# Gated attention and mixture of experts on one core: the order of ranking, indexed stores and first products

## The chip, the cores and the metric

The kernel runs on one core of a Trainium2 chip. The metric is the time of one execution in microseconds (us) of the device, the median of several runs. Engines go by the names of the profile: PE (TensorE matmuls), PEld (its weight loads), DVE (VectorE), ACT (ScalarE), POOL (GpSimd) and SP (SyncE, which here only issues DMAs). Each engine works through its own list of instructions in order; it stops at an instruction whose inputs or whose buffer are not ready, and everything behind it in that list stops too.

## The reference

For 4 batches and 8 heads, 768 steps, a state of 48 x 48 is decayed and read:

```python
f = 1.0 / (1.0 + np.exp(-f_logit))
for t in range(S):
    state = f[:, :, t, :, None] * state + np.einsum('bhd,bhe->bhde', k[:, :, t], v[:, :, t])
    y[:, :, t] = np.einsum('bhd,bhde->bhe', q[:, :, t], state)
```

Its 3072 rows of 384 numbers go to a mixture of 8 experts with 1024 hidden units:

```python
logits = x @ w_gate                       # 8 logits a row
expert_idx = np.argmax(logits, axis=1)    # one expert a row
for i in range(N):                        # in the order of the rows
    e = expert_idx[i]
    if counts[e] < capacity:
        disp[e, counts[e]] = x[i]; pos[i] = counts[e]; counts[e] += 1; keep[i] = True
h = np.maximum(np.einsum('ecd,edf->ecf', disp, w1), 0.0)
y = np.einsum('ecf,efd->ecd', h, w2)
out[i] = gate_w[i] * y[expert_idx[i], pos[i]]   # for the rows kept, gate_w the softmax weight
```

## The kernel before, in words

**Attention in slots.** The 3072 rows are 24 blocks of 128, six to a batch. A prologue readies the first ones, then slots 0 to 24 follow. The order within a slot is written by hand and holds for all five engines. In slot `n`, in this order:

- `keys_pe(n)` turns the keys of block `n` (PE, psT buffers), ACT copies them out as `kn`; `y_out` copies the result of block `n-1` (ACT).
- `scores_pe(n+1)` (PE, psA), which ACT copies to `AT` and POOL masks with two affine selects.
- `kq_pad(n+3)` copies loaded keys and queries into a padded tile `kqp` (POOL in slots 0 to 6, ACT later); `kq_in(n+2)` transposes them (PE, psT), and DVE multiplies them by decays into `kT` and `qT`.
- `f_in` transposes the gates of two blocks in every odd slot (PE, two psF buffers, one for each block). In slots 9 and 15 it stands behind `inter`, otherwise ahead of it.
- `inter(n)` (PE) reads the carried state `S`; `update(n)` (PE) makes the new one, which DVE adds up (`U`) and POOL decays into the next `S` (`carry`).
- `decay(n+3)` and `decay_back(n+3)` are two scans on DVE over the psF buffer of block `n+3`. The second one writes `Rq`, and the buffer is free when it ends.
- `rows_pe(n-1)` (PE) turns the result into rows with the 8 logits beside them, as products with `identc`, which holds an identity and the gate columns; ACT copies them into a ring of 12 blocks.
- `values(n)` (PE) adds the block's own part.

`load` issues on SP the transfers of k and q together (`kq`, three buffers), of v, and of f for two blocks. `late_constants` loads the gate columns into `identc` with four small DMAs, and the capacity.

**Ranking.** The rows of a group of blocks (`GROUPS`) are given their expert together: POOL adds partial logits (`choose_sum`), DVE finds the largest (`choose_max`) in the slot after the group's last block is in rows; one slot later POOL multiplies by `desc`, DVE finishes the one-hot choice (`choose_first`, into `tally`), PE ranks the rows with matmuls of ones and a triangle (`rank_pe`), and DVE makes from that the row numbers `ri` (`pick` and `put`). The first two groups have six blocks each, the others three or one.

**Stores by index.** `flush_scatter` sends one ranked block of 128 rows to the experts' buffer `disp` in HBM: an indirect DMA that POOL issues. `SCATTERS` says how many a slot; `AHEAD` names four slots that have one more, ahead of the masks. From slot 20 on one more follows each `rows_copy`. The rows of blocks 0 to 14 for expert 0 are read back first: after the store of block 14, SP loads `xg0`.

**The first expert inside attention.** In the last slots `early_prep` transposes `xg0` (PE, psF), and ACT and DVE split it into `x0h` and `x0l`. `early_pe` makes the eight first-layer products of 256 rows (nine matmuls each; psF for most, psT for two, psA for the last) and `early_out` takes them out (`hh` on ACT, then `hl` on DVE). The table `EARLY` says in which slot, and at which of three places in it. The second layer follows, then a second small expert and seven sorted by size, with the weights of each loaded and split meanwhile. `QUARTERS` says where POOL splits parts of the first expert's weights (`w1l`).

The functions that the diff touches:

## Time and profile before

| what | value |
|---|---|
| runs | 384.35, 383.87, 384.09 us; median 384.09 |
| profiled execution | 385.96 us; span from first to last instruction 383.5 us |
| instructions | 10139 |
| PE busy | 371.7 us, 97% of the span |
| DVE busy | 212.2 us, 55% |
| ACT busy | 201.9 us, 53% |
| POOL busy | 178.7 us, 47% |
| granted PE clock | 0.998 |

The profile is of one execution, and all durations in this text are of that one. A row of its timeline has the start in us, the length, the engine and source line, the operation with output and inputs, how many were merged into the row, and in brackets how long the engine sat idle just before and which instruction's end released it. The ends of matmuls are modelled: a PE that waits inside a group of matmuls can look busy. Slots are told apart by `rows_pe`, line 539: that of slot 1 starts at 22.76, of slot 7 at 51.79, of slot 13 at 81.28, of slot 19 at 113.38. The first matmul of the second layer (line 1019) starts at 143.88.

### The profile page before, as it was taken

The page shows a single profiled execution, that of the slowest core. Times are in us where ns is not written, and L with a number is a line of the kernel's source. Part 1 is how long each engine was busy: PE and PEld are TensorE (multiplying, and loading weights), DVE is VectorE, ACT ScalarE, POOL GpSimd, SP SyncE. Part 2 cuts the span into 40 slices and gives each one's busy share as a digit, 9 for nine tenths or more (in the row PEclk, how much of TensorE's full clock was granted, in tenths as well). Part 3 has the DMA queues.
Part 4 walks back from the last instruction along what each step waited for, and adds up shares of the span by engine and source line. Part 5 has one row for each costly group of instructions (what it writes and reads, how often), then busy time and mean ns, then how long its engine had stood idle before and what let it go on. Part 6 is the DMA issues. An engine that isn't in the chain of part 4 may idle for free.

```text
span 383.5 us, 10139 instructions
## 1 busy us (share of the span) xinstructions
PE 371.7 (97%) x4007; PEld 347.1 (91%) x4007; DVE 212.2 (55%) x482; ACT 201.9 (53%) x425; POOL 178.7 (47%) x260
## 2 busy tenths in 40 slices
PE   8889999999999999999999999999999999999994
PEld 7789899888878899998899989999999999999994
DVE  4988889878889867534943343225225235222310
ACT  3556668876768632552834553545454464462311
POOL 6664545677767853254253430370290281292012
PEclk9999999999999999999999999999999999999999
DMA  8979999999883423679386174175156036211001
GB/s 154 213 156 225 230 241 228 242 226 248 205 228 101 146 97 120 231 220 321 126 273 195 29 243 124 43 239 180 42 184 227 23 125 210 76 60 41 16 22 40
DMA packets 83323, 60.87 MB, mean 159 GB/s; under 512 B 65671, under 2 KB 77829, under 8 KB 83268
## 3 DMA queue, kind: packets, MB, share of 16 engines
q1 hardware_dynamic: 79476, 50.13, 50.6%
q0 software_dynamic: 3520, 9.92, 6.9%
q8 instruction: 33, 0.54, 0.6%
q14 instruction: 22, 0.18, 0.2%
q10 hardware_dynamic: 272, 0.10, 0.1%
HBM read 49.42 MB, written 11.43 MB: 159 GB/s over the span
## 4 chain that ended last, share of the span: by engine, by line
PE 74%; issue 9%; DMA 5%; POOL 4%; SPq 3%; ACT 3%; DVE 1%; POOLq 1%; ACTq 0%
PE psM L1190 15%; PE psA L763 11%; PE psM L763 9%; PE psM L1019 7%; PE psA L539 5%; PE psY L518 5%; PE psA L420 5%; PE psY L464 3%; DMA raw<-in_moe_w_dram 3%; PE psA L484 2%; PE psT L360 2%; PE psT L447 2%; PE psT L1161 2%; PE psF L763 2%; PE psF L360 1%
## 5 line engine op out<-in xcount | busy, mean ns | idle before, releaser
L320 POOL DMA_INDIRECT out_dram<-yo,g_ti x30 | 30.0, 998 | 100.5 <-ACT yo L1206 40.3
L144 POOL TENSOR_TENSOR w2l<-raw,w2h 128x768 fp32r<-128x768 f32 x28 | 51.2, 1856 | 39.4 <-ACT w2h L135 39.4
L770 DVE SCALAR_TENSOR_TENSOR hl<-psA,hh 128x224 fp32r<-128x224 f32 (+8 forms) x33 | 18.5, 559 | 48.6 <-ACT hh L769 48.6
L144 DVE TENSOR_TENSOR w1l<-raw,w1h 128x1024 fp32r<-128x1024 f32 x21 | 25.5, 1223 | 24.5 <-ACT w1h L135 24.5
L135 ACT ACTIVATE w1h<-raw 128x1024 fp32r<-128x1024 f32 x24 | 25.3, 1062 | 25.4 <-DMA raw<-in_moe_w_dram 25.3
L1019 PE MATMUL psM<-w2h,hh 128*128 128x384 f32 (+2 forms) x112 | 37.6, 342 | 0.0
L1019 PE MATMUL psM<-w2l,hh 128*128 128x384 f32 (+2 forms) x112 | 37.5, 338 | 0.0
L1019 PE MATMUL psM<-w2h,hl 128*128 128x384 f32 (+2 forms) x112 | 37.4, 337 | 0.0
L770 DVE SCALAR_TENSOR_TENSOR hl<-psM,hh 128x224 fp32r<-128x224 f32 (+7 forms) x32 | 17.8, 562 | 31.1 <-ACT hh L769 31.1
L1190 PE MATMUL psM<-hh,w2h 128*128 128x440 f32 (+3 forms) x96 | 34.1, 355 | 0.0
L1190 PE MATMUL psM<-hl,w2h 128*128 128x440 f32 (+3 forms) x96 | 34.1, 355 | 0.0
L1190 PE MATMUL psM<-hh,w2l 128*128 128x440 f32 (+3 forms) x96 | 33.8, 352 | 0.0
L430 POOL TENSOR_SCALAR_AFFINE_SELECT AT<-AT 128x512 f32<-128x512 f32 x48 | 29.4, 636 | 8.5 <-ACT AT L426 8.3
L135 ACT ACTIVATE w2h<-raw 128x768 fp32r<-128x768 f32 x32 | 27.1, 847 | 9.9 <-DMA raw<-in_moe_w_dram 8.7
L320 POOL DMA_INDIRECT disp<-rows,ri x24 | 25.6, 1065 | 13.1 <-issue 3.5
L380 DVE TENSOR_TENSOR_SCAN Suf<-psF,direv 112x511 f32<-112x511 f32 x24 | 29.1, 1211 | 3.8 <-PE psF L360 3.8
L769 ACT ACTIVATE hh<-psA 128x224 fp32r<-128x224 f32 (+8 forms) x33 | 16.2, 492 | 27.1 <-PE psA L763 20.5
L763 PE MATMUL psM<-xh,w1h 128*128 128x480 f32 (+6 forms) x84 | 29.7, 354 | 0.0
L763 PE MATMUL psA<-xh,w1h 128*128 128x480 f32 (+6 forms) x84 | 29.7, 353 | 0.1
L763 PE MATMUL psM<-xl,w1h 128*128 128x480 f32 (+6 forms) x84 | 29.7, 354 | 0.0
L763 PE MATMUL psA<-xh,w1l 128*128 128x480 f32 (+6 forms) x84 | 29.4, 350 | 0.0
L394 DVE TENSOR_TENSOR_SCAN Rq<-psF,d 112x512 f32<-112x512 f32 x24 | 29.4, 1224 | 0.0
(238 smaller groups left out, 958.6 us busy)
## 6 DMA issues: line engine op xcount, KB each, us to landing
raw<-in_moe_w_dram SPq DMA_DIRECT2D x24, 512.0 KB
raw<-in_moe_w_dram SPq DMA_DIRECT2D x32, 384.0 KB
ld_kq<-in_k_dram SPq DMA_DIRECT2D x24, 192.0 KB
ld_kq<-in_q_dram SPq DMA_DIRECT2D x24, 192.0 KB
ld_v<-in_v_dram SPq DMA_DIRECT2D x24, 192.0 KB
ld_f<-in_f_logit_dram SPq DMA_DIRECT2D x11, 384.0 KB
xg<-disp SPq DMA_DIRECT2D x6, 589.5 KB
xg<-disp SPq DMA_DIRECT2D x3, 393.0 KB
```

The costliest lines, as they stand in the source:

```text
L135: return nc.scalar.activation(hi, raw, AF.Copy)
L144: engine.tensor_tensor(lo[cs], raw[cs], hi[cs].bitcast(F32), op=ALU.subtract)
L320: ins = nc.gpsimd.indirect_dma_start(out=dst, out_offset=bass.IndirectOffsetOnAxis(ap=idx, axis=0), in_=rows, in_offset=None, bounds_check ...
L380: nc.vector.tensor_tensor_scan(out=_view(Suf[:R], m - 1, [[-1, m]]), data0=_view(F, m, [[-1, m]]), data1=_view(direv[:R], m - 1, [[-1, m]] ...
L394: nc.vector.tensor_tensor_scan(out=Rq[:R], data0=F, data1=d1[:R], initial=0.0, op0=ALU.mult, op1=ALU.max)
L420: nc.tensor.matmul(pas[s][:, p], kTs[n][r, p], qTs[n][r, p], start=True, stop=True)
L430: nc.gpsimd.affine_select(AT[:, s], AT[:, s], pattern=[[0, NP], [1, C]], compare_op=ALU.is_ge, fill=0.0, base=0, channel_multiplier=-1)
L518: nc.tensor.matmul(py[b][64 * g : 64 * g + m, a, :], vt[:, 2 * p + s, :m], AT[:, s, p, :], start=(first(n) and a == 0), stop=(a == NP // 2 ...
L763: nc.tensor.matmul(ph[:, :T], a[:, c, fs], x[:, c, :T], start=(n == 0), stop=(n == 3 * DT - 1))
L770: nc.vector.scalar_tensor_tensor(out=hl[:, :T], in0=ph[:, :T], scalar=0.0, in1=hh[:, :T].bitcast(F32), op0=ALU.max, op1=ALU.subtract)
L1019: nc.tensor.matmul(py[:n], x[:, ks], a[:, ft], start=(ft == 0 and m == 0), stop=(ft == FT - 1 and m == 2))
L1190: nc.tensor.matmul(pys[c][:, :T], a[:, ft, cs], x[:, :T], start=(ft == 0 and n == 0), stop=(ft == FT - 1 and n == 2))
```

## The change

The first twelve blocks are ranked in three groups of four. Blocks are stored one a slot from slot 7 on (two in slot 20), and the extra stores ahead of the masks are gone. The load of `xg0` stands a slot later, and with it the transposes and products of the first expert. In slot 0 the copy of key and query block 3 goes behind `carry`, `f_in(4)` ahead of `kq_in(3)` in slot 1, the gate columns are loaded earlier and the capacity later.

```diff
-    GROUPS = ((0, 6), (6, 6), (12, 3), (15, 3), (18, 3), (21, 1), (22, 1), (23, 1))
-    RT = 6
+    GROUPS = ((0, 4), (4, 4), (8, 4), (12, 3), (15, 3), (18, 3), (21, 1), (22, 1), (23, 1))
+    RT, RING = 4, 12
...
-    QUARTERS = {9: (0, 3), 12: (0, 1), 13: (1, 2), 14: (1, 2), 20: (2, 3), 21: (2, 1)}
-    SCATTERS = {9: 1, 10: 1, 11: 1, 12: 1, 13: 1, 14: 1, 15: 1, 16: 1, 17: 1, 18: 2, 19: 1, 20: 0}
-    AHEAD = (15, 17, 19, 21)
+    QUARTERS = {9: (0, 1), 10: (0, 1), 11: (0, 2), 12: (1, 2), 15: (1, 2), 18: (2, 2), 21: (2, 2)}
+    SCATTERS = {n: 1 for n in range(NT - 3)}
...
         for s in range(2):
-            copied = nc.scalar.activation(AT[:, s], pas[s], AF.Copy)
-        if n - 1 in AHEAD:
-            flush_scatter(copied.ins)
+            nc.scalar.activation(AT[:, s], pas[s], AF.Copy)
...
     def rows_parts(n, px):
-        t, c = divmod(n, RT)
-        if t not in parts_of:
-            parts_of[t] = abuf.tile([P, RT, NP, NE], F32, name="parts", bufs=1)
-        nc.scalar.activation(parts_of[t][:, c], px[:, :, 2 * D :], AF.Copy)
+        nc.scalar.activation(ring_parts[:, n % RING], px[:, :, 2 * D :], AF.Copy)
...
     EARLY = {
-        (NT - 3, 1): ((early_prep, 0),),
-        (NT - 3, 2): ((early_prep, 1), (early_prep, 2)),
-        (NT - 2, 0): ((early_pe, 0), (early_pe, 1)),
...
+        (NT - 2, 0): ((early_prep, 0),),
+        (NT - 2, 1): ((early_prep, 1),),
+        (NT - 2, 2): ((early_prep, 2),),
+        (NT - 1, 0): ((early_pe, 0), (early_pe, 1)),
...
     def prologue():
...
         load("v", 1)
+        late_constants()
         keep_busy(4)
...
         load("v", 2)
-        late_constants()
         load("kq", 5)
...
     def loads_of(n):
         load("v", n + 3)
-        if n < PAD_ACT:
+        if 0 < n < PAD_ACT:
             load("kq", n + 6)
         if n == 0:
             load("f", 4)
+        if n == 2:
+            nc.sync.dma_start(cap_i, capacity.bitcast(I32).partition_broadcast(P))
...
     def slot(n):
...
-        if fn and n < PAD_ACT:
+        if 0 < n < PAD_ACT:
             kq_pad(n + 3)
...
+        if n == 1:
+            f_in(4)
         if kqn:
             kq_in(n + 2)
...
-        if n == 1:
-            f_in(4)
         loads_of(n)
...
         if keyed:
             carry(n)
+        if n == 0:
+            kq_pad(3)
+            load("kq", 6)
...
-        if n == NT - 5:
+        if n == NT - 4:
             ins = nc.sync.dma_start(xg0, dispv[0, : T_FIRST[0]].rearrange("(k p) w -> p k w", p=P))
```

**POOL and SP in slots 0 and 1.** The rows of POOL from the copy of block 2 (into `kqp0`) to the masks of AT(2); `S1` is the state that `inter(1)` reads. Before:

```order
L401 COPY kqp0_122<-ld_kq2_105 128x16x48
L430 AFFINE_SELECT AT_346<-AT_346 128x512 x2
L401 COPY kqp1_124<-ld_kq0_103 128x16x48
L430 AFFINE_SELECT AT_417<-AT_417 128x512 x2
L504 TENSOR_TENSOR S1_149<-U_438,pendall_189 112x4x48
L401 COPY kqp0_122<-ld_kq1_104 128x16x48
L430 AFFINE_SELECT AT_503<-AT_503 128x512 x2
```

After:

```order
L399 COPY kqp0_122<-ld_kq2_105 128x16x48
L426 AFFINE_SELECT AT_351<-AT_351 128x512 x2
L426 AFFINE_SELECT AT_416<-AT_416 128x512 x2
L500 TENSOR_TENSOR S1_149<-U_435,pendall_189 112x4x48
L399 COPY kqp1_124<-ld_kq0_103 128x16x48
L399 COPY kqp0_122<-ld_kq1_104 128x16x48
L426 AFFINE_SELECT AT_512<-AT_512 128x512 x2
```

The copy of block 3 (into `kqp1`) has moved from in front of the masks of AT(1) to behind the state. On SP the gate columns move ahead of `kq` 4 (buffer 1) and `v` 2, and the capacity goes to slot 2. Before, from the load of v 1 on:

```order
L199 DMA ld_v1_108<-in_v_dram 128x8x48
L204 DMA ld_kq1_104<-in_k_dram 64x8x96
L204 DMA ld_kq1_104<-in_q_dram 64x8x96
L199 DMA ld_v2_110<-in_v_dram 128x8x48
L276 DMA identc_151<-in_moe_w_gate_dram 48x2x8 x4
L277 DMA cap_i_168<-in_moe_capacity_dram 128x2
L204 DMA ld_kq2_105<-in_k_dram 64x8x96
```

After:

```order
L198 DMA ld_v1_108<-in_v_dram 128x8x48
L275 DMA identc_151<-in_moe_w_gate_dram 48x2x8 x4
L203 DMA ld_kq1_104<-in_k_dram 64x8x96
L203 DMA ld_kq1_104<-in_q_dram 64x8x96
L198 DMA ld_v2_110<-in_v_dram 128x8x48
L203 DMA ld_kq2_105<-in_k_dram 64x8x96
```

**DVE from slot 9 to slot 10.** From the second scan of block 12 (`Rq`) to that of block 13, whose end frees the psF buffer for `f_in` of slot 11. Before:

```order
L394 SCALAR_TENSOR_TENSOR Rq_1478<-psF_1425,d1_145 112x512
L409 TENSOR_TENSOR kT_1532<-psT_1514,Suf0_141 112x512
L409 TENSOR_TENSOR qT_1534<-psT_1515,Rq_1478 112x512
L498 TENSOR_TENSOR U_1562<-psA_1553,S0_147 112x192
L380 SCALAR_TENSOR_TENSOR Suf1_143<-psF_1426,direv_138 112x511
L388 RECIPROCAL d1_145<-Suf1_143 112x4
L389 TENSOR_TENSOR pendall_189<-psF_1426,Suf1_143 112x4
L394 SCALAR_TENSOR_TENSOR Rq_1585<-psF_1426,d1_145 112x512
```

After, with the choice of blocks 4 to 7 in front of kT:

```order
L392 SCALAR_TENSOR_TENSOR Rq_1481<-psF_1430,d1_145 112x512
L575 TENSOR_REDUCE r_m_1483<-rows_195 128x4
L577 TENSOR_TENSOR r_w_1485<-rows_195,r_m_1483 128x32
L583 TENSOR_REDUCE r_wm_1522<-r_w_1485 128x4
L585 TENSOR_TENSOR tally_1118<-r_w_1485,r_wm_1522 128x32
L407 TENSOR_TENSOR kT_1543<-psT_1525,Suf0_141 112x512
L407 TENSOR_TENSOR qT_1545<-psT_1526,Rq_1481 112x512
L494 TENSOR_TENSOR U_1580<-psA_1564,S0_147 112x192
L634 TENSOR_TENSOR r_sel_1582<-psA_1564,tally_1118 128x4x8
L378 SCALAR_TENSOR_TENSOR Suf1_143<-psF_1431,direv_138 112x511
L386 RECIPROCAL d1_145<-Suf1_143 112x4
L387 TENSOR_TENSOR pendall_189<-psF_1431,Suf1_143 112x4
```

Four instructions of the choice and one of the ranking now stand between the two scans, as they did in slots 8 and 14 before.

**PE at the end of slot 22.** `tally` in the last columns is the choice of block 21. Before, from the end of the third product of the first expert to the start of the fourth:

```order
L763 MATMUL psF<-x0l,w1h 128x256
L763 MATMUL psF<-x0h,w1l 128x256
L677 LDWEIGHTS onesb
L677 MATMUL psT<-base_178,onesb 128x8
L678 LDWEIGHTS onesb
L678 MATMUL psT<-tally,onesb 128x8
L684 LDWEIGHTS tri
L684 MATMUL psT<-tally,tri 128x8
L960 LDWEIGHTS onesb
L960 MATMUL psT<-flb,onesb 128x1
L763 MATMUL psF<-x0h,w1h 128x256
```

After, from the end of `values(22)`:

```order
L514 MATMUL psY<-AT,ld_v_114 64x128
L710 MATMUL psF<-ident,xg_85 128x128 x2
L667 LDWEIGHTS onesb
L667 MATMUL psT<-base_178,onesb 128x8
L668 LDWEIGHTS onesb
L668 MATMUL psT<-tally,onesb 128x8
L674 LDWEIGHTS tri
L674 MATMUL psT<-tally,tri 128x8
L947 LDWEIGHTS onesb
L947 MATMUL psT<-flb,onesb 128x1
L745 MATMUL psF<-x0h,w1h 128x256
```

Between `values(22)` and this ranking there is now a pair of transposes of `xg0` where there was a product of nine matmuls, and the first product comes behind the ranking.

More of the change, by code (lines that the diff above doesn't have):

```diff
@@ L276, in late_constants @@
                 nc.sync.dma_start(identc[64 * g : 64 * g + D, b::2, 2 * D :], gates_of[b, g ^ b])
-        nc.sync.dma_start(cap_i, capacity.bitcast(I32).partition_broadcast(P))
     ohc = const.tile([P, NE], BF16, name="ohc")
@@ L412 @@
     MS = (64, D)
-    pus, ATs, kns, pys, yTs, marks, parts_of = {}, {}, {}, {}, {}, {}, {}
+    pus, ATs, kns, pys, yTs, marks = {}, {}, {}, {}, {}, {}
     def scores_pe(n):
@@ L541, in rows_pe @@
         return px
-    ring = abuf.tile([P, 2 * RT, W], F32, name="rows", bufs=1)
+    ring = abuf.tile([P, RING, W], F32, name="rows", bufs=1)
     def row_at(n):
-        return ring[:, n % (2 * RT)]
+        return ring[:, n % RING]
     def rows_at(g, m):
-        c = g % (2 * RT)
+        c = g % RING
         return ring[:, c : c + m]
     def rows_copy(n, px):
-        if n >= 2 * RT:
+        if n >= RING:
             nc.gpsimd.tensor_copy(row_at(n)[:, DM + NE : W], tokid[:, n : n + 1])
@@ L560, in rows_copy @@
         marks[n].append(m)
+    ring_parts = abuf.tile([P, RING, NP, NE], F32, name="parts", bufs=1)
     def rows_parts(n, px):
[L563 to L566 removed]
+        nc.scalar.activation(ring_parts[:, n % RING], px[:, :, 2 * D :], AF.Copy)
     def group(g, m):
[L569 to L570 removed]
+        c = g % RING
+        return ring_parts[:, c : c + m], rows_at(g, m)[:, :, DM : DM + NE]
     def choose_sum(g, m):
@@ L593, in sum_parts @@
     def sum_parts(g, m):
-        t, c = divmod(g, RT)
-        nc.vector.tensor_reduce(
-            out=rows_at(g, m)[:, :, DM : DM + NE],
-            in_=parts_of[t][:, c : c + m].rearrange("r c a e -> r c e a"),
-            axis=AX.X,
-            op=ALU.add,
-        )
+        part, L = group(g, m)
+        nc.vector.tensor_reduce(out=L, in_=part.rearrange("r c a e -> r c e a"), axis=AX.X, op=ALU.add)
     def rows_logits(n, px):
@@ L687, with flush_scatter @@
     queue, early_ins, slot_now, ri_of = [], [], {"n": 0}, {}
-    def flush_scatter(behind=None):
+    def flush_scatter():
         if queue:
@@ L693, in flush_scatter @@
             ins = scatter(disp, ri_of.pop(n), row_at(n), NV * RPE - 1, ("disp", "late") if late else ("disp",))
-            if behind is not None:
-                tc.add_manual_dep(
-                    ins,
-                    behind.name,
-                    mybir.DependencyInfo(mybir.DependencyClass.Sync, mybir.DependencyReason.DATA),
-                    reason="not during the transposes",
-                )
             if not late:
@@ L740 @@
     EARLY = {
-        (NT - 3, 1): ((early_prep, 0),),
-        (NT - 3, 2): ((early_prep, 1), (early_prep, 2)),
-        (NT - 2, 0): ((early_pe, 0), (early_pe, 1)),
-        (NT - 2, 1): ((early_out, 0), (early_out, 1)),
-        (NT - 2, 2): ((early_pe, 2),),
-        (NT - 1, 0): ((early_out, 2), (early_pe, 3)),
-        (NT - 1, 1): ((early_out, 3), (early_pe, 4)),
-        (NT - 1, 2): ((early_out, 4), (early_pe, 5)),
-        (NT, 0): ((early_out, 5),),
-        (NT, 2): ((early_pe, 6), (early_pe, 7), (early_out, 6)),
+        (NT - 2, 0): ((early_prep, 0),),
+        (NT - 2, 1): ((early_prep, 1),),
+        (NT - 2, 2): ((early_prep, 2),),
+        (NT - 1, 0): ((early_pe, 0), (early_pe, 1)),
+        (NT - 1, 1): ((early_out, 0), (early_pe, 2)),
+        (NT - 1, 2): ((early_out, 1), (early_out, 2), (early_pe, 3), (early_pe, 4)),
+        (NT, 0): ((early_out, 3), (early_pe, 5)),
+        (NT, 1): ((early_out, 4),),
+        (NT, 2): ((early_pe, 6), (early_pe, 7), (early_out, 5), (early_out, 6)),
     }
@@ L845, in slot @@
             pas = scores_pe(n + 1)
-        if fn and n < PAD_ACT:
+        if 0 < n < PAD_ACT:
             kq_pad(n + 3)
         if n == 3:
-            nc.gpsimd.tensor_copy(ring[:, :, DM + NE : W], tokid[:, : 2 * RT].unsqueeze(2))
+            nc.gpsimd.tensor_copy(ring[:, :, DM + NE : W], tokid[:, :RING].unsqueeze(2))
         while half:
```

2 lines of the change are left out of this document (removed).

## The prediction

> **What bounds the kernel now.** I first read the busy time of TensorE in four stretches of the span, to learn whether an engine or a wait sets the end. Columns: stretch, its length, then busy time and instructions of PE, PEld, DVE, ACT and POOL, granted clock, DMA share, GB/s.
>
> ```profile
> 23.50:144.00 120.50, 117.96 (x2406) 105.18 (x2402) 102.01 (x223) 84.35 (x210) 77.39 (x128) 1.00 0.86 203
> 144.00:200.00 56.00, 55.91 (x335) 52.08 (x335) 32.00 (x103) 27.00 (x54) 22.75 (x20) 1.00 0.66 217
> 200.00:330.00 130.00, 130.00 (x715) 124.69 (x714) 49.27 (x97) 64.16 (x112) 45.65 (x33) 1.00 0.44 142
> 46.62:75.75 29.13, 28.80 (x641) 25.96 (x641) 25.97 (x50) 23.50 (x57) 16.22 (x28) 1.00 1.07 235
> 75.75:107.41 31.66, 30.52 (x648) 26.79 (x648) 27.41 (x58) 23.29 (x57) 23.98 (x42) 1.00 0.97 231
> ```
>
> From the end of attention (144 us) TensorE is busy without a gap, so whatever moves that moment moves the end of the kernel by as much; the change edits nothing behind it. Before it TensorE is missing 2.5 us in the open and more inside its groups: slots 13 to 18 (last row) hold the same work as slots 7 to 12 (the row above), but for 0.2 us of ranking, and take 2.53 us longer. So I read the timeline of attention engine by engine, and take each part of the change by one question: does TensorE arrive earlier or later at its next instruction.
>
> **Part 1, slots 0 and 1.** Four places in the timeline of slot 1, and the DMA engines' busy tenths from 20 to 40 us in steps of 0.5 us:
>
> ```profile
> 21.05 0.67 PE L464 MATMUL psY<-qT,S 48*64 48x128 f32 x16 [0.54 <-POOL S L504]
> 22.76 0.93 PE L539 MATMUL psA<-identc,yT 112*64 112x104 f32 x16 [0.45 <-DMA identc<-in_moe_w_gate_dram]
> 18.53 0.83 POOL L401 COPY kqp<-ld_kq 128x768 f32<-128x768 f32 x1 [3.01 <-DMA ld_kq<-in_q_dram]
> 18.02 2.36 SPq L276 DMA_DIRECT2D identc<-in_moe_w_gate_dram  x4
> 20.42 1.54 SPq L277 DMA_DIRECT2D cap_i<-in_moe_capacity_dram  x1
> DMA  5310000699999999999999992696599999999999
> 26.80 0.69 DVE L409 TENSOR_TENSOR kT<-psT,Suf 112x512 f32<-112x512 f32 x1 [1.39 <-PE psT L360]
> ```
>
> TensorE waits 0.54 us for the carried state S, because POOL first copies `kq` block 3 (0.83, itself released only by its DMA) and masks AT. It waits 0.45 us more for the gate columns, whose four small loads SP issues at 18.02. SP spends 3.9 us on these and the capacity, while the DMA engines run dry from 20.5 to 23.5. The change issues the gate loads three loads earlier, moves the capacity to slot 2, and puts the copy of block 3 behind S; `f_in(4)` fills TensorE while that copy runs. Both waits go: -1.0, and I take -1.1 for the shorter queue. What is pushed back: `kq` 4 and `v` 2 go behind the four gate loads (2.36 us), so POOL's copies of blocks 3 and 4 now stand together in front of AT(2); these are needed only in slot 2, where VectorE has 1.39 us idle (last row), and the filled DMA hole gives the time back. `kq` 6 now waits for the copy of block 3 and stands behind `f` 4, a load of 384 KB more; its copy is due in slot 3, and the same hole covers it. If that cover fails, half the gain goes: from -1.2 to -0.4.
>
> **Part 2, groups of four.** Three groups issue 18 ranking matmuls for 16, at 0.04 us: +0.1. What matters is VectorE. The chain that chooses an expert is now in front of kT in slots 6, 10 and 14 (before: 8 and 14). In slots 9 and 15 the code puts the next transposes of f behind `inter`; slots 7 and 11, which now follow a choice, keep them ahead. They write two psF banks, and the second is free when Rq of the slot before ends. Rows: Rq(8), kT(8), Rq(9) and the transposes of slot 7, then the same of slots 10 and 11, then the choice in slot 8 from its first to its last instruction.
>
> ```profile
> 43.49 1.22 DVE L394 TENSOR_TENSOR_SCAN Rq<-psF,d 112x512 f32<-112x512 f32 x1
> 45.60 0.69 DVE L409 TENSOR_TENSOR kT<-psT,Suf 112x512 f32<-112x512 f32 x1 [0.89 <-PE psT L360]
> 48.53 1.22 DVE L394 TENSOR_TENSOR_SCAN Rq<-psF,d 112x512 f32<-112x512 f32 x1
> 50.15 0.61 PE L360 MATMUL psF<-ident,pf 64*112 64x64 f32 x16
> 64.03 1.22 DVE L394 TENSOR_TENSOR_SCAN Rq<-psF,d 112x512 f32<-112x512 f32 x1
> 65.60 0.69 DVE L409 TENSOR_TENSOR kT<-psT,Suf 112x512 f32<-112x512 f32 x1 [0.35 <-PE psT L360]
> 68.63 1.22 DVE L394 TENSOR_TENSOR_SCAN Rq<-psF,d 112x512 f32<-112x512 f32 x1
> 69.75 0.81 PE L360 MATMUL psF<-ident,pf 64*112 64x64 f32 x16
> 54.95 0.17 DVE L580 TENSOR_REDUCE r_m<-rows 128x6 f32<-128x48 f32 x1
> 55.16 0.21 DVE L582 TENSOR_TENSOR r_w<-rows,r_m 128x48 f32<-128x48 f32 x1
> 56.01 0.38 DVE L590 TENSOR_TENSOR tally<-r_w,r_wm 128x48 bf16<-128x48 f32 x1
> 45.32 0.82 POOL L401 COPY kqp<-ld_kq 128x768 f32<-128x768 f32 x1 [2.70 <-PE psA L420]
> 83.90 1.41 POOL L144 TENSOR_TENSOR w1l<-raw,w1h 128x256 fp32r<-128x256 f32 x2
> 84.66 0.73 DVE L582 TENSOR_TENSOR r_w<-rows,r_m 128x48 f32<-128x48 f32 x1
> ```
>
> The choice takes 56.39 - 54.95 = 1.44 us. In slot 10 it starts at 65.25 (end of Rq) and ends at 66.7, where kT(12) stood at 65.60: 1.1 late. With r_sel (0.1) Rq(13) ends 1.2 later, at 71.0; the transposes of slot 11 already wait for it (0.81 us against 0.61 in slot 7), so TensorE loses nearly all of it. I take +1.0 (shorter operands), ends 0.5 and 1.4. In slot 6 VectorE has more air: 44.71 + 1.44 = 46.15 against 45.60, Rq(9) ends at 50.4 and the transposes stood at 50.15: +0.2. The upper end is 1.0, if POOL's copy of block 9 (45.32, after 2.70 us of waiting) still stands in front of POOL's share of the choice. Slot 14 chooses as before.
>
> One rule bears on this chain. Its first two-input instruction took 0.21 us, and 0.73 in slot 14, while POOL ran w1l. The Trainium skill (SBUF — State Buffer, Who interferes with whom) says a VectorE instruction with two SBUF inputs is blocked whole by a GpSimd one that reads SBUF; the trace agrees. By it slot 10, whose choice starts under a quarter of w1l, would lose 0.5 more, and the total below would be 387.1.
>
> **Part 3, stores by index.** 24 stores stay 24, each about 1.0 us of POOL, now one a slot from 7 on in place of pairs in slots 15 and 17 to 19. POOL's masks are needed a slot later and hide them. The twelve quarters of w1l that POOL splits (1.41 us for two, above) move with them to slots where POOL is not asked for a choice in the next; they are due at the first product, in slot 22 or later, and cost nothing. So does the one ring for the partial logits, twelve blocks deep like the rows. If crowding costs part of the 2.53 us above, some comes back: -0.3, ends -1.3 and +0.4.
>
> **Part 4, the first expert a slot later.** Rows in order: the store of token block 14 and the load of xg0 behind it; S in slot 20; the transposes of xg0 and the first product; slot 22 from `inter` to the third product; VectorE's split of x0 and its last choice step in slot 22; then slot 23.
>
> ```profile
> 116.22 1.02 POOL L320 DMA_INDIRECT disp<-rows,ri  x1 [0.17 <-issue]
> 119.03 0.37 SPq L953 DMA_DIRECT2D xg<-disp  x1
> 119.94 0.51 POOL L504 TENSOR_TENSOR S<-U,pendall 112x192 f32<-112x192 f32 x1 [0.99 <-DVE r_sel L644]
> 122.80 0.44 PE L727 MATMUL psF<-ident,xg 128*128 128x128 f32 x2
> 125.37 0.66 PE L727 MATMUL psF<-ident,xg 128*128 128x128 f32 x4
> 127.69 0.38 PE L763 MATMUL psF<-x0h,w1h 128*128 128x256 f32 x1 [0.32 <-issue]
> 130.04 0.67 PE L464 MATMUL psY<-qT,S 48*64 48x128 f32 x16
> 133.19 0.39 PE L763 MATMUL psF<-x0h,w1h 128*128 128x256 f32 x1
> 127.21 0.75 DVE L729 TENSOR_TENSOR x0l<-psF,x0h 128x256 fp32r<-128x256 f32 x2
> 133.34 0.23 DVE L633 TENSOR_SCALAR tally<-r_w,r_wm 128x8 bf16<-128x8 f32 x1
> 137.09 0.42 DVE L770 SCALAR_TENSOR_TENSOR hl<-psF,hh 128x256 fp32r<-128x256 f32 x1 [0.18 <-issue]
> 138.35 1.05 PE L518 MATMUL psY<-AT,ld_v 128*64 128x128 f32 x16
> 139.16 0.19 DVE L603 TENSOR_REDUCE rows<-psA 128x8 f32<-128x32 f32 x1 [1.64 <-PE psA L539]
> 140.04 0.23 DVE L633 TENSOR_SCALAR tally<-r_w,r_wm 128x8 bf16<-128x8 f32 x1
> ```
>
> The store of block 14 becomes the second of slot 20. POOL is free at 120.45; two stores with the copy of a token number between them end at 123.0. The load was issued 119.03 - 117.24 = 1.8 behind the store's end, so now at 124.8. It landed at most 3.8 after its issue (the transposes at 122.80 did not wait), at least the 1.8 a store takes; I take 2.8, half way: 127.6. TensorE comes there at 127.37 (first product less its 0.32 wait) less the moved transposes (0.44 + 0.66): 126.3. It waits 1.3, between 0.3 and 2.3. Queued behind it: `inter`, `update` and the rank of blocks 18 to 20.
>
> Next is the rank of block 21. TensorE reaches it at 127.6 + 0.4 + 3.15 (from 130.04 to 133.19) + 0.6 for two transposes = 131.7; before, the third product (1.2 us) stood in front of it. VectorE has the one-hot at 133.57 less 1.1, the splits of x0 that are gone ahead of it (the two in place of hl cost the same): 132.4. That is +0.6 (0 to 1.3; larger where the load is earlier). In slot 23 the fourth product needs the psF bank of the second, and its hl now stands behind the choice. Counted from rows(22): choice done at 140.27, hl at 140.7, TensorE ready at 139.4: 1.3; TensorE's end there is modelled 0.64 before VectorE saw it, so at least 0.65: I take +0.8. The product in psT waits likewise, +0.2 (0 to 0.4). The 0.32 ahead of the first product goes: -0.3. Together +2.6.
>
> **Sum.** -1.1 + 0.1 + 0.2 + 1.0 - 0.3 + 2.6 = +2.5. The profiled execution took 385.96 us, 1.87 over the median of the runs, for a span of 383.5; it would become 388.5, the span 386.0, the median 384.09 + 2.5 = 386.6.
>
> **Rivals.**
> - Crowded stores were the bound (faster). Slots 13 to 18 lose 2.53 us against 7 to 12. For: the pairs fall in these slots. Against: 13, 14 and 16 have one store each and lose too, and slots 9 to 12, with one each, do not. If the even spacing recovers that and as much again per slot in 19 and 20 (3.4 in all), the time is 386.6 - 3.1 = 383.5, or 383.0 with the best of part 1; it decides from 2.8 us recovered. Chance 0.22. The Trainium skill (SBUF — State Buffer, Who interferes with whom) says that TensorE and ScalarE never wait for a port; by that no store could hold TensorE up directly.
> - The tail is covered (no change). The load lands 1.8 behind its issue and VectorE is early; part 4 then costs 0.5 and the time is 384.5. For: VectorE is the emptier engine there. Against: four waits have to go at once. Chance 0.16.
> - The load is late (slower still). At 3.8 behind its issue, and with the copy of block 9 late in slot 6, 1.0 + 0.8 more: 388.4. Chance 0.12.
> - The stalls of slots 7 and 11 do not exist, since the psF banks alternate otherwise: 385.4. This stays within my forecast.
>
> **How the numbers follow.** The forecast, 385.2 to 387.8, has 0.50; with the late load, slower by over 0.2% (about what a measurement of this kernel can tell) has 0.62. The covered tail gives 0.16 to no change, the stores 0.22 to faster. The range reaches from 383.2, inside the rival of the stores, to 388.2.
>
> **What would show it.** In slot 1 no wait for S or the gate columns. In slots 7 and 11 the f transposes stretched to some 0.8 and 1.8 us. At the first transposes of xg0, in slot 22, an idle TensorE of about 1.3 us released by the load; another ahead of the rank of block 21 and of the fourth product. Slots 13 to 18 still near 31.4 us. Wrong: if xg0 lands within 2 us of its issue, or if slots 13 to 20 become as short as 7 to 12.

## The result, and the profile after

| | before | after |
|---|---|---|
| time, median of 4 runs | 384.22 us | 388.98 us (388.33 to 389.93) |
| ratio, 95% interval | | 1.0125 (1.010 to 1.015) |
| profiled execution, span | 385.96, 383.5 us | 389.20, 387.1 us |
| first matmul of the second layer | 143.88 us | 147.29 us |

The change costs 4.8 us; the forecast was 2.5, and 388.98 lies above its range. Single executions of one kernel spread by 1% and more on these chips, and a profiled one can lie far over its kernel's median (396.92 against 392.23 us in e8, 390.77 against 386.06 in e6, 392.65 against 388.68 in e5), so in what follows a verdict is a ratio with its interval, and a row of a trace is what one execution did. The two profiled executions here differ by 3.2 us and not by 4.8, because that of before lay 1.87 over its median.

The stretches of the changed kernel that answer to those of before: attention, two stretches behind it, slots 7 to 12 and 13 to 18 (slot n runs from the start of `rows_pe` of slot n-1 to that of slot n), and three more in the last slots. Columns as before; the granted clock stands ahead of the last two.

```profile
21.85:147.29 125.44, 120.32 (x2428) 107.72 (x2423) 104.26 (x234) 83.94 (x209) 79.23 (x134) 0.97 0.83 195
147.29:200.00 52.71, 52.71 (x320) 49.05 (x319) 30.18 (x95) 25.39 (x50) 22.55 (x19) 1.00 0.64 208
200.00:330.00 130.00, 130.00 (x715) 124.73 (x714) 50.11 (x103) 64.89 (x113) 45.88 (x35) 1.00 0.46 150
46.16:76.31 30.15, 29.11 (x641) 26.04 (x639) 27.11 (x55) 23.27 (x56) 18.66 (x30) 1.00 1.07 240
76.31:105.61 29.30, 29.00 (x645) 26.16 (x645) 26.75 (x58) 23.25 (x57) 20.99 (x39) 1.00 1.06 237
123.80:126.42 2.62, 0.02 (x2) 0.00 (x0) 1.98 (x8) 1.29 (x4) 0.00 (x0) 1.00 0.73 229
126.42:134.00 7.58, 7.58 (x82) 6.23 (x83) 3.30 (x11) 2.14 (x5) 6.71 (x10) 0.55 0.45 160
134.00:147.29 13.29, 12.62 (x143) 11.47 (x141) 7.33 (x27) 5.18 (x15) 5.02 (x9) 1.00 0.20 77
```

Behind attention TensorE is busy without a gap, as before, and of the 3.6 us by which the span grew 3.4 are there when attention ends. Inside attention three things stand out. Slots 13 to 18 take 29.3 us where before they took 31.66. At 123.8 TensorE stands idle for 2.6 us. And behind that its granted clock is 0.55 for 7.6 us, the only such place while TensorE has work.

Where time was won and lost is read from the starts of `rows_pe`, the same matmuls in both kernels. The second profile of before is of another execution, taken later (b2_before below); the length of a stretch stands in each column.

```
stretch (start of rows_pe of slot)     before  before again  after   after - before
start to slot 5                         41.97         43.22  41.26   -0.71
slot 5 to slot 12                       33.78         34.24  35.05   +1.27
slot 12 to slot 21                      47.82         45.45  44.30   -3.52
slot 21 to the second layer             20.31         20.08  26.68   +6.37
```

So two of the four stretches got faster, by 4.2 us together, and the last three slots alone took back more. (0.37 us of the third and fourth row is the first pair of transposes of `xg0`, which moved past `rows_pe` of slot 21.) Against the second profile of before the four differences are -2.0, +0.8, -1.2 and +6.6: the loss in the last slots is the same, the gain in slots 13 to 21 shrinks to a third (see b2_before). In slot 1 both waits are gone, as the first two rows show; slots 6, 7, 10 and 11 of the changed kernel are these:

```profile
20.85 0.67 PE L460 MATMUL psY<-qT,S 48*64 48x128 f32 x16
21.95 0.89 PE L535 MATMUL psA<-identc,yT 112*64 112x104 f32 x15
44.26 0.82 POOL L399 COPY kqp<-ld_kq 128x768 f32<-128x768 f32 x1 [1.20 <-DMA ld_kq<-in_q_dram]
45.33 0.19 DVE L583 TENSOR_REDUCE r_wm<-r_w 128x4 f32<-128x32 f32 x1 [1.03 <-POOL r_w L581]
50.15 0.66 PE L358 MATMUL psF<-ident,pf 64*112 64x64 f32 x15 [0.33 <-DVE r_sel L639]
66.53 0.32 PE L480 MATMUL psA<-ld_v,kn 128*48 128x48 f32 x5 [0.27 <-issue]
70.21 0.92 PE L358 MATMUL psF<-ident,pf 64*112 64x64 f32 x16
```

The choice of slot 6 waits 1.03 us for POOL, whose copy of block 9 waited 1.20 for its load. The transposes of f wait 0.33 in slot 7, and in slot 11 take 0.92 where they took 0.81. Slot 10 has its ranking (0.24) and, in the middle of `update`, 0.27 us of "issue", idle time for which the profile shows no cause. Slots 10 and 11 together take 10.14 us where they took 9.19, slots 6 and 7 10.47 where they took 9.72, and slot 8, which has no choice any more, 4.60 where it took 5.08.

The last slots, from the store of block 14 (the second row; the first is that of block 13) to the fourth product; the third row is the last work of TensorE ahead of the transposes of `xg0`:

```profile
118.06 1.02 POOL L318 DMA_INDIRECT disp<-rows,ri  x1 [0.22 <-issue]
119.44 0.98 POOL L318 DMA_INDIRECT disp<-rows,ri  x1 [0.16 <-issue]
122.70 1.12 PE L418 MATMUL psA<-qT,kT 48*128 48x128 f32 x16
123.40 0.37 SPq L940 DMA_DIRECT2D xg<-disp  x1
126.42 0.44 PE L710 MATMUL psF<-ident,xg 128*128 128x128 f32 x2 [2.61 <-DMA xg<-disp]
126.65 1.01 POOL L318 DMA_INDIRECT disp<-rows,ri  x1 [3.60 <-DMA xg<-disp]
126.79 1.11 PE L460 MATMUL psY<-qT,S 48*64 48x128 f32 x16
130.28 1.42 POOL L143 TENSOR_TENSOR w1l<-raw,w1h 128x256 fp32r<-128x256 f32 x2
131.65 1.22 POOL L426 TENSOR_SCALAR_AFFINE_SELECT AT<-AT 128x512 f32<-128x512 f32 x2
131.84 1.05 DVE L620 SCALAR_TENSOR_TENSOR r_w<-rows,r_m,desc 128x8 f32<-128x8 f32 x1
140.48 0.39 PE L745 MATMUL psF<-x0h,w1h 128*128 128x256 f32 x1 [0.67 <-DVE hl L752]
```

The load is issued 2.98 us behind the end of the store it waits for, where before it was 1.79, and lands 3.02 behind its issue; TensorE has had nothing else to do since 123.8 and waits 2.61 for it. POOL waits too: its next store is released by the load's landing, after 3.60 us. The 16 matmuls of `inter` then take 1.11 us where they took 0.67. TensorE reaches the rank of block 21 so late that the choice of that block, whose two-input step takes 1.05 us under the masks that POOL runs behind its two quarters of w1l, holds nobody up here. The fourth product waits 0.67 for `hl`.

The page shows the clock in one line, in 40 slices of the span:

```profile
PEclk9999999999999699999999999999999999999999
```

### The profile page after: what moved, and what is told of

It reads as the page before. It is cut to its first block, busy times and chain, and to the rows that moved or that the text cites. A ratio compares the mean times of both kernels' runs of the same rounds, so it can differ in the third digit from the quotient of the medians.

```text
span 387.1 us, 10152 instructions
## 1 busy us (share of the span) xinstructions
PE 374.4 (97%) x4009; PEld 350.6 (91%) x4009; DVE 212.4 (55%) x490; ACT 201.4 (52%) x425; POOL 178.5 (46%) x263
## 4 chain that ended last, share of the span: by engine, by line
PE 71%; issue 9%; DVE 8%; DMA 4%; POOL 4%; SPq 2%; ACT 1%; POOLq 1%; DVEq 0%
PE psM L1177 14%; PE psA L745 12%; PE psM L745 11%; PE psM L1006 9%; PE psA L418 3%; PE psA L535 3%; PE psY L514 2%; DMA ld_kq<-in_q_dram 2%; PE psT L1148 2%; DVE Rq L392 2%; DVE Suf L378 2%; PE psF L358 2%; PE psY L460 2%; PE psA L368 2%; PE psF L745 2%
## 5 line engine op out<-in xcount | busy, mean ns | idle before, releaser
L318 POOL DMA_INDIRECT disp<-rows,ri x24 | 24.2, 1007 | 17.1 <-DVE tally L645 5.6
```

Source lines behind the costliest of these rows:

```text
L318: ins = nc.gpsimd.indirect_dma_start(out=dst, out_offset=bass.IndirectOffsetOnAxis(ap=idx, axis=0), in_=rows, in_offset=None, bounds_check ...
```

## The experiments

All times are compared with runs of before on the same chip. Beside the ratio stands, where it helps, the difference of the median spans: the time around the span is no constant here, see the last section.

### Was the profile of before typical?

**b2_before**, the kernel before unchanged.

> The kernel before once more, for its profile. Slots 13 to 21 took 47.8 us from the rows of block 11 to those of block 20 in the profile shown, 44.3 in the changed kernel. Theory A, a good part of this is the one execution's own (it lay 1.87 us over the median): here they take 46 us or less. Theory B, the order of before costs it every time: 47.4 to 48.2.

45.45 us: theory A. The profile on which the prediction rests carried 2.4 us of its own in slots 13 to 21. Against this one the changed kernel gains 1.15 us there, 0.37 of it the moved transposes. The other traces of the experiments below, by the chip on which they were taken, in us for slots 13 to 21:

| chip | stores in the order of before | stores one a slot |
|---|---|---|
| 6 | 44.79 (e4, its transposes moved as well) | 44.29 (e3), 44.29 (c1), 44.31 (c2) |
| 14 | 45.45 (b2) | 44.94 (e5) |
| 8 | 47.20 (e11), 47.73 (e9), 47.82 (e10) | 47.18 (e8, in an execution 4.7 us over its median) |

With the 0.37 taken off where the transposes have not moved, the two orders lie within 0.5 us of each other on every chip, while the chips lie up to 3 us apart. (With pairs of stores in two slots, e1, e2, e6, e7 and c3 took 45.56 to 46.15 on chips 6 and 14.) So the 3.5 us between the first two profiles are not shown to come from the order of the stores. On which chips those two were taken is not known, and why these slots take longer on chip 8 was not found.

### What the last slots cost

**e4_tail_new**, part 4 alone, in the kernel before:

```diff
-        (NT - 3, 1): ((early_prep, 0),),
...
+        (NT - 2, 0): ((early_prep, 0),),
...
-        if n == NT - 5:
+        if n == NT - 4:
             ins = nc.sync.dma_start(xg0, ...)
```

> The kernel before with only the load, transposes and products of the first expert a slot later. Its store of block 14 is out in slot 19, so the load is issued near 119 us as it was or a little later, and no wait for it is due. Theory A, the load's lateness was the cost: 384.9 (384.2 to 385.4), the rest being the wait for hl ahead of the fourth product. Theory B, the place of the products is the cost: 386.5 to 389.

1.000 (0.997 to 1.003), 385.36 us beside 385.09; in the span +1.25. Theory B is out, and the span rose by about what theory A leaves for the rest. From slot 21 to the second layer it took 22.09, 1.4 more than before without the moved transposes. TensorE does not wait for `xg0` at all: the store of block 14 stands alone in slot 19 here and the load is issued at 117.83. It waits for the choice of block 21 and for `hl`, as forecast. The waits of TensorE from 119 to 148 us, in e4_tail_new (columns: engine, tile, line, releaser; total us, times, longest):

```profile
PE psT L684 <- DVE tally L633: 0.9, 1, 0.9
PE psF L762 <- DVE hl L769: 0.7, 1, 0.7
```

**e2_load_early**, the changed kernel with the load of `xg0` a slot earlier; for that the store of block 14 has to be out sooner:

```diff
-    SCATTERS = {n: 1 for n in range(NT - 3)}
+    SCATTERS = {n: 1 + (n in (15, 18)) for n in range(NT - 3)}
...
-        if n == NT - 4:
+        if n == NT - 5:
```

> The changed kernel with its transposes and products a slot later as they are, but the load of xg0 issued a slot earlier as before, and two stores in slots 15 and 18. Theory A, only the late load and the fall of the clock behind it cost: no idle TensorE ahead of the transposes of xg0, the granted clock stays at 1.0, and the time is that of e1_tail_old plus 0.7 for the wait for hl ahead of the fourth product: about 382. Theory B, the later products cost by themselves (fewer matmuls to cover the choice of the last blocks): 384 to 386.

1.0089 (1.005 to 1.013), 389.24 us, span +4.9: theory A fell, the loss is hardly smaller, and it is larger than theory B has it. The idle time ahead of the transposes is gone, and another took its place, at the rank of block 21. TensorE, VectorE's step of that choice, and POOL in e2_load_early:

```profile
132.98 0.17 PE L674 MATMUL psT<-tally,tri 128*128 128x8 bf16 x1 [2.05 <-DVE tally L623]
130.69 1.77 DVE L620 SCALAR_TENSOR_TENSOR r_w<-rows,r_m,desc 128x8 f32<-128x8 f32 x1
129.84 1.43 POOL L143 TENSOR_TENSOR w1l<-raw,w1h 128x256 fp32r<-128x256 f32 x2
131.21 1.22 POOL L426 TENSOR_SCALAR_AFFINE_SELECT AT<-AT 128x512 f32<-128x512 f32 x2
```

A step of 0.23 us takes 1.77: it starts under POOL's quarters of w1l and ends with its masks. In e4_tail_new, with one quarter in slot 21, the same step took 0.23. The Trainium skill (SBUF — State Buffer, Who interferes with whom) says that a VectorE instruction with two SBUF inputs contends with a GpSimd one that reads SBUF, for ports that it calls an exclusive lock; the traces agree, with 0.23 us for this step in e4, e5 and e8 against 0.39 (e6) to 1.77 where it meets POOL's quarters or masks.

**e3_busy**, the changed kernel with TensorE kept busy during the wait, by matmuls that nothing reads:

```diff
+    def early_busy(m):
+        pw = psF.tile([P, P], F32, name="psF")
+        for _ in range(m):
+            nc.tensor.matmul(pw, ident, ident, start=True, stop=True)
...
-        (NT - 2, 0): ((early_prep, 0),),
+        (NT - 2, 0): ((early_busy, 9), (early_prep, 0)),
```

> The changed kernel with nine idle matmuls of the identity, some 2.2 us, ahead of the first transposes of xg0, where TensorE waited 2.6 us for the load. Theory A, the granted clock of 0.55 from 126.4 to 134 us is the answer to this idle time and costs about 2 us: the clock stays at 1.0 and the time falls to 387.0 (386.5 to 387.6). Theory B, the clock falls for another reason, or the slots behind the load wait for other engines anyway: 388.5 to 389.5, as without.

1.0102 (1.006 to 1.015). The clock stays at 1.0 behind the load, and TensorE comes to the rank of block 21 early enough to be stopped there for 2.17 us; then the clock falls. In that choice the two-input step takes 0.60 us, and the last step, line 623, takes 1.59 where e2 has 0.24; it too ends with POOL's masks. Theory A had the answer of the clock right and the time wrong; theory B's second half holds: with the first stall covered, the second one shows. Slots 10 and 11 take 10.14 us here as well, and as TensorE is not held up in slot 10, it waits in slot 11 where the forecast had it, for the scan behind the choice:

```profile
70.78 0.66 PE L358 MATMUL psF<-ident,pf 64*112 64x64 f32 x15 [0.51 <-DVE Rq L392]
```

**e5_quarters20** and **e6_load_quarters**: the last two quarters of w1l go to slot 20, in the changed kernel and in e2_load_early.

```diff
-    QUARTERS = {..., 18: (2, 2), 21: (2, 2)}
+    QUARTERS = {..., 18: (2, 2), 20: (2, 2)}
```

> The changed kernel with the last two quarters of w1l in slot 20 in place of 21, nothing else. Theory A, GpSimd's quarters in slot 21 block VectorE's choice of block 21, and TensorE waits for that at its rank whenever the load of xg0 has not stopped it longer before: the choice runs unblocked (its two-input step 0.23 us, not 1.05), the load still stops TensorE 2.6 us: the time falls by 0 to 1.5 us, to 387.5 to 389.0 where before has 384.2. Theory B, the quarters are off the path: 389.0 as it was.

> e2_load_early (load of xg0 issued a slot earlier, two stores in slots 15 and 18) with the last two quarters of w1l in slot 20 in place of 21. Theory A, the blocked choice of block 21 cost 1.2 us of waiting and as much again of low clock behind it: TensorE waits under 1 us ahead of the rank of block 21, as in e4_tail_new, the clock stays up, and the time falls 2.4 us against e2_load_early, to 386.5 (385.9 to 387.2) where before has 384.2 to 385.1. Theory B, TensorE waits for VectorE's choice without regard to GpSimd: 388.5 to 389.5.

| | quarters in slot 21 | quarters in slot 20 |
|---|---|---|
| load late | after: 1.0125 (1.010 to 1.015) | e5: 1.0132 (1.008 to 1.018) |
| load early | e2: 1.0089 (1.005 to 1.013) | e6: 1.0052 (1.003 to 1.008) |

From slot 21 to the second layer the four took 26.68, 26.72, 24.66 and 21.78 us. Moving the quarters alone gains nothing, moving the load alone 2.0 in this stretch, both 4.9. The two stalls stand one behind the other, and whichever comes first hides the other. For e6 theory A holds: the ratio gives 386.2 us, and the clock stays up in the last slots. In e6 TensorE waits 0.68 us for the choice:

```profile
133.84 0.17 PE L674 MATMUL psT<-tally,tri 128*128 128x8 bf16 x1 [0.68 <-DVE tally L623]
```

e6 is still 0.5% slower than before; its trace has the wait for `hl` (0.68), the pairs of stores (see e1) and slot 6. There the upper end of the forecast came true, and more, in an execution of 390.77 us. TensorE's ranking, VectorE's step ahead of it, and POOL in slot 6 of e6_load_quarters:

```profile
47.71 0.22 PE L671 MATMUL psA<-tally,onesb 128*128 128x24 bf16 x3 [1.57 <-DVE tally L585]
47.06 0.19 DVE L583 TENSOR_REDUCE r_wm<-r_w 128x4 f32<-128x32 f32 x1 [2.59 <-POOL r_w L581]
45.99 0.82 POOL L399 COPY kqp<-ld_kq 128x768 f32<-128x768 f32 x1 [3.48 <-DMA ld_kq<-in_q_dram]
```

POOL's copy waits 3.48 us for a load, its share of the choice stands behind it, VectorE waits 2.59 for that and TensorE 1.57; the clock answered with 0.50 here too.

**e8_busy20**, e5_quarters20 with the nine idle matmuls of e3_busy, then **c1_quarters20** and **c2_busy20**, e5 and e8 again, side by side on one chip.

> e5_quarters20 (the changed kernel with the last quarters of w1l in slot 20) with nine idle matmuls of the identity ahead of the first transposes of xg0. TensorE still reaches the transposes no earlier than the load, but it is busy until then, and nothing blocks the choice of block 21 behind it. Theory A, the fall of the granted clock behind the wait is a cost of its own: the clock stays at 1.0 to the end of attention and the time falls by 1.5 to 2.5 us against e5_quarters20, to 386.2 to 387.2 where before has 383.8 to 384.2. Theory B, the wait is the whole cost and the low clock is hidden: 388 to 389.

> e5_quarters20 once more, beside c2 on one chip. Theory A and B alike: TensorE waits about 2.5 us for xg0, then a granted clock near 0.5 until TensorE has been busy for some 6 us; rows of slot 21 to the end of attention take 26.7 us; 1.010 to 1.015 of before.

> e8_busy20 once more, beside c1. Theory A, the low clock is a cost of its own, beside the wait: the clock stays at 1.0, rows of slot 21 to the end of attention take 24.5 to 25.0 us, and the time is 1.5 to 2.2 us under c1's. Theory B, TensorE would wait for other engines in that stretch anyway: within 0.5 us of c1.

e8: 1.0113 (1.009 to 1.013), 392.23 us on a chip where before took 387.38; beside e5's ratio that is no difference that could be told, as theory B has it. c1: 1.0153 (1.011 to 1.020), 391.24 us; c2: 1.0105 (1.007 to 1.015), 388.76 us, 2.5 us less, as theory A has it, though the intervals overlap. The two traces do not show this gain in the last slots: they are 3.18 us apart at the second layer, but 3.06 already at slot 12. They do show why the loss varies. Granted clock in steps of 2 us behind the load, c1_quarters20 (the column ahead of the last two):

```profile
127.00:129.00 2.00, 0.00 (x0) 0.00 (x0) 1.90 (x8) 1.04 (x3) 0.08 (x1) 1.00 0.96 283
129.00:131.00 2.00, 1.95 (x36) 1.45 (x36) 0.61 (x4) 0.72 (x1) 1.43 (x2) 0.91 0.94 337
131.00:133.00 2.00, 2.00 (x28) 1.88 (x27) 1.40 (x6) 0.67 (x3) 1.83 (x4) 0.50 0.49 177
133.00:135.00 2.00, 2.00 (x25) 1.81 (x22) 1.34 (x5) 0.58 (x2) 1.83 (x4) 0.74 0.30 107
```

What is missing to full clock sums to (0.09 + 0.50 + 0.26) x 2 = 1.7 us here, where c1's expectation has a low clock for some 6 us. In the changed kernel it is 7.58 x 0.45 = 3.4; in e5, from 126 us on, 3.4; in e2 and e3 1.7. The clock goes to half for one stretch of about 3.4 us, which loses 1.7 us, or for two, which lose 3.4. e5 and c1 are the same kernel: with two stretches the way from slot 21 to the second layer takes 26.72 us (26.68 in the changed kernel), with one 25.02. Of these 1.7 us 0.26 are a longer wait for `xg0`, 2.40 against 2.14. In c2 no clock falls, but TensorE waits 1.29 us for the choice, whose step took 1.27 under POOL's masks alone, so it saves only 0.14 against c1 in these two executions. So the low clock is a cost of its own, 1.4 to 1.7 us a stretch in these traces, where TensorE has no other wait to meet; what keeping the clock up is worth in time is not settled: the pairs differ by 0.7 us (e5 and e8, by their ratios) and 2.5 (c1 and c2). The Trainium skill (TensorE: Matmul & The Clock Gate, Part 1) says that the array is gated to half its clock after an idle window of about 3.4 us and needs as long a busy one to come back. The half and the stretches of 3.4 us agree; waits of 2.6, 2.1 and, in slot 6 of e6, 1.57 us were enough here, shorter than such a window, while one of 1.29 in c2 was not.

**c3_hl_ahead**, e6 with pairs of stores in slots 16 and 19 and the second product's `hl` ahead of the choice of block 22:

```diff
-        (NT - 1, 1): ((early_out, 0), (early_pe, 2)),
-        (NT - 1, 2): ((early_out, 1), (early_out, 2), (early_pe, 3), (early_pe, 4)),
+        (NT - 1, 1): ((early_out, 0), (early_out, 1), (early_pe, 2)),
+        (NT - 1, 2): ((early_out, 2), (early_pe, 3), (early_pe, 4)),
```

> e6_load_quarters with the pairs of stores in slots 16 and 19 and with the second product's hl ahead of the choice of block 22 on VectorE. Theory A, the fourth product waits for that hl because of its place: the 0.67 us of waiting go, rows of slot 23 to 24 take 5.4 where they took 6.07, and the time is 0.5 to 0.7 us under e6_load_quarters, 1.003 to 1.004 of before. Theory B, the choice comes later by as much and the rank of block 22 waits instead: 1.005 as there.

1.003 (1.000 to 1.006). Slot 23 to 24 takes 5.33 us where it took 6.08, and no other wait takes its place: theory A by the trace. The ratio is as forecast too, but its interval reaches over e6's, and the pairs moved as well.

### The other parts

**e1_tail_old**, the changed kernel with `EARLY` and the load as before and two stores in slots 15 and 18; **e7_old_tail2**, the same with the pairs in slots 16 and 19, the last quarters in slot 20, and

```diff
-        if n % 2 and fn and n not in (1, 9, 15):
+        if n % 2 and fn and n not in (1, 11, 15):
...
-        if n in (9, 15):
+        if n in (11, 15):
             f_in(n + 3, n + 4)
```

> The changed kernel with the first expert's load, transposes and products back in the slots of before, and two stores in slots 15 and 18 (the other slots one), so that the store of token block 14 is out in slot 19. Theory A, the load of xg0 came after TensorE was ready for it and everything won before slot 21 was thrown away in that wait: rows of block 21 stay about 3 us earlier than before and nothing is given back behind them: 381.2 us (380.6 to 381.8). Theory B, the two pairs of stores alone cost TensorE about half a microsecond each: 382.2. Theory C, the last slots lose their time whatever the place of the load: 385 or more.

> e1_tail_old with its two pairs of stores in slots 16 and 19, where no quarters of w1l run, the last quarters in slot 20, and the transposes of f behind inter in slots 11 and 15, which follow a choice (they were in 9 and 15). Theory A, what e1_tail_old lost to its pairs (0.6 us in each of slots 17 and 20) and to the scan ahead of the transposes of slot 11 (0.5 to 0.9) comes back: 1.2 to 2 us under e1_tail_old, 382.4 to 383.4 where before has 384.2. Theory B, the pairs cost wherever they stand: 384 to 385.

e1: 1.0009 (0.998 to 1.004); e7: 1.0024 (0.999 to 1.006). Without part 4 the change is no loss in time, but no gain either; the spans rose by 1.4 and 1.25 us. All three theories of e1 miss: its ratio gives 384.6, above A and B and under C. From slot 21 both run 19.90 and 19.91 us, about as before (20.31 and 20.08). Slots 13 to 21 take 45.94 and 45.95 us, and the pairs cost 1.3 of it: slot 17 takes 5.43 and slot 20 5.65 where the changed kernel needs 4.80 and 5.01, and the same 5.42 and 5.65 with the pairs one slot later. Theory B of e7 holds. The new place of the transposes of f cannot be judged: e7 spent 1.9 us on "issue" in slot 10.

**e10_slot0**, the new order of slots 0 and 1 alone, in the kernel before; **e9_slot0_quarters**, that and the quarters of slot 13 in slot 14.

```diff
-    QUARTERS = {9: (0, 3), 12: (0, 1), 13: (1, 2), 14: (1, 2), 20: (2, 3), 21: (2, 1)}
+    QUARTERS = {9: (0, 3), 12: (0, 1), 14: (1, 4), 20: (2, 3), 21: (2, 1)}
```

> The kernel before with the new order of slots 0 and 1 alone. Theory A: no wait for S or the gate columns in slot 1, and the rows of slot 5 come 0.9 to 1.1 us earlier, which stays: 382.7 to 383.1 where before has 383.8. Theory B, the waits come back as waits for kq in slots 2 to 6: 383.6 to 384.

> The kernel before with the new order of slots 0 and 1, and with the two quarters of w1l of slot 13, which stand in front of the choice of blocks 6 to 11, moved to slot 14; groups, stores and the last slots as before. Theory A, these are the parts that gain: 0.9 from slots 0 to 5 and 0.5 to 0.9 from slots 13 and 14: 382.3 to 382.9 where before has 383.8. Theory B, the gain of slots 0 and 1 is taken back by the loads of keys and queries by slot 9: 383.2 to 384.

e10: 0.9960 (0.994 to 0.998), 385.93 us beside 387.38: faster than before, and the version to keep: theory A by the time. Part 1 is worth 1.5 us (0.6 to 2.4). The waits of slot 1 that it removes are 0.99 us in the profile shown, but 1.11 (e4), 1.45 (e11) and 1.71 (b2) in the other traces with the old order. Slot 5, which was to come an us earlier, ends at 42.42 in this trace; over all traces that point lies at 41.97 to 43.22 us in four with the old order and at 40.77 to 42.42 in thirteen with the new one, 0.8 earlier on average. Part of it is taken back in that trace, though: S waits for POOL in slot 2, behind a copy that is itself late by its load. TensorE and POOL in e10_slot0:

```profile
27.15 0.67 PE L463 MATMUL psY<-qT,S 48*64 48x128 f32 x16 [0.99 <-POOL S L503]
24.62 0.83 POOL L400 COPY kqp<-ld_kq 128x768 f32<-128x768 f32 x1 [4.74 <-DMA ld_kq<-in_q_dram]
```

e9: 0.9975 (0.9955 to 0.9995). The quarters moved out of slot 13 show no gain: slots 13 to 15 took 5.43, 5.66 and 5.55 us, where e10, with the quarters in place, has 5.69, 5.65 and 5.13. The expected 0.5 to 0.9 is a miss, and theory B is the nearer one.

**e11_groups**, groups of four alone, with the stores from slot 9 on:

```diff
-    GROUPS = ((0, 6), (6, 6), (12, 3), ...)
-    RT = 6
+    GROUPS = ((0, 4), (4, 4), (8, 4), (12, 3), ...)
+    RT, RING = 4, 12
...
-    QUARTERS = {9: (0, 3), 12: (0, 1), ...}
-    SCATTERS = {9: 1, ...}
+    QUARTERS = {9: (0, 1), 11: (0, 2), 12: (0, 1), ...}
+    SCATTERS = {7: 0, 8: 0, 9: 1, ...}
```

> The kernel before with the first twelve blocks ranked in three groups of four, the stores from slot 9 on as before; the three quarters of w1l in slot 9, which would stand in front of the choice of slot 10, are one in slot 9 and two in slot 11. Theory A, the choice of slot 6 waits on GpSimd behind the copy of key and query block 9, which waits for its DMA, and the transposes of slot 11 wait for Rq: slot 6 becomes 0.5 to 1.8 longer, slots 10 and 11 together 0.5 to 0.9, and the time rises by 1 to 2 us, to 385 to 386 where before has 383.8. Theory B, groups of four cost only their two ranking matmuls more: 383.8 to 384.2.

1.0003 (0.998 to 1.003), the span +0.9. Slots 5 to 12 take 35.18 us, 1.4 more than in the first profile of before and 0.9 more than in the second. By the trace theory A in the main (slot 6 0.3 longer, slots 10 and 11 1.0), by the time theory B: what the span loses comes back around it, and the interval leaves both open. In the twelve traces with groups of four slots 6 to 12 took 34.31 to 40.59 us, in the five without 33.77 to 34.84. The four longest of the twelve (e5, e6, c3 and e8, 37.53 and more) are executions about 4 us and more over their medians, and most of what they took longer lies in slots 6, 7, 10 and 11; why is open.

## Why the prediction was wrong

| step | forecast | what the runs showed |
|---|---|---|
| part 1, slots 0 and 1 | -1.1 | both waits gone; -0.71 by slot 5, -1.5 alone (e10). Right |
| part 2, slots 6 to 11 | +1.3 | +1.27 in slots 6 to 12 (+0.81 against b2). Slots 10 and 11 +0.95 for +1.0, but the transposes of slot 11 took 0.92, not the 1.8 named, because TensorE came later out of slot 10. Slots 6 and 7 +0.75 for +0.2, and slot 8, which the sum leaves out, -0.48: right in the sum, in part by luck. In e6 slot 6 alone took 1.8 more |
| part 3, stores | -0.3 | -3.5 against the profile shown, -1.2 against b2, within 0.5 either way on one chip. Not contradicted |
| part 3, quarters | 0 | 1.4 of waiting, and 1.7 lost to the low clock behind it, when the load is early (e2 against e6). Failed |
| part 4, wait for `xg0` | +1.3 | 2.61, and 3.4 lost to the low clock behind it. Failed |
| part 4, rank, `hl`, the rest | +1.3 | 0.86 + 0.67 of waits in e4, the span +1.25. Right; in the changed kernel only the 0.67 for `hl` shows |

The step that failed is the wait for `xg0`: "at 124.8", "I take 2.8, half way: 127.6", "It waits 1.3". The prediction lets the store of block 14 end at 123.0, has the load issued 1.8 behind that and landed another 2.8 later, and TensorE ready at 126.3. The store ended at 120.42 and TensorE was ready at 123.82, both 2.5 us earlier, since slots 13 to 21 were shorter than in the profile of before; the distance of the two was right, 3.4 for 3.3. What was wrong is the length of the chain between them: the load was issued 2.98 behind the store's end and landed 3.02 later, 6.0 us where the sum has 4.6, and this 1.4 makes a wait of 2.6 out of one of 1.3. The rival of the late load had nearly this chain (5.6), but put the lateness into the landing, and it was the issue. The issue term was read from a store that stands alone, and in the change this store follows right behind another. In seven traces where it does (after, e3, e5, e8, c1, c2, c3) the load was issued 3.68 to 4.10 us behind the start of the store, in nine where it stands alone 2.75 to 3.05; but in e7, where it is the second of a pair too, it was 2.88, so the cause stays open.

Second, the wait was priced by its length alone, and the granted clock behind it was put at nothing. From the landing of `xg0` to the rank of block 21 the forecast has 131.7 - 127.6 = 4.1 us; it took 133.49 - 126.42 = 7.07, nearly all at half clock, and so TensorE met no wait there. To the second layer the forecast has 146.4 - 127.6 = 18.8 us; it took 147.29 - 126.42 = 20.87, and what is missing to full clock (3.4) is more than that difference, because the wait for the choice is hidden by it. Of the 6.37 us that the last slots lost, 2.61 are the wait, 3.4 the clock, 0.67 the wait for `hl` and 0.37 the moved transposes; the 0.32 ahead of the first product went, and 0.4 is left over.

Third, "they are due at the first product, in slot 22 or later, and cost nothing". That looks at when the quarters are needed and not at whom they block. The same rule that the prediction applied to slot 10, where the quarter had ended 0.1 us before and the step took 0.19, held in slot 21, where it was not applied. As e5 shows, it changes nothing in the kernel as it is, since the late load hides it; it is why an earlier load alone does not repair it.

Last, the sum was made against a profiled execution whose slots 13 to 21 were 2.4 us slower than another one's. The text gave its distance from the median, 1.87 us, and did not ask where in the kernel it lay. Slots 13 to 18 came to 29.30 us, not to the 31.4 that the prediction named, and no longer than slots 7 to 12 (30.15), which it gave as a sign of being wrong. That does not make its rival of the crowded stores right: with the stores of before, b2 has 30.28 beside 29.59 in these slots too. The 2.53 us on which that rival stood were for the most part one execution's own.

## What to carry to other kernels

Where TensorE waits for a chain through other engines, here a store of POOL, the load that SP issues behind it and its landing, price the whole chain, from more than one row, and from a row in which the store stands as it will stand. Price a wait of TensorE of some 2 us at more than its length when the granted clock falls behind it, and look for the second stall that the first one hides: two repairs that each gain little may gain together. Where single executions differ by 1%, take a second profile of the kernel before and see in which stretch the two differ, before a gain or a loss is put down to the order of the instructions, and compare traces of one chip.
